# A gated mix of sliding-window attention and a GEGLU on one core: keys of the first two chunks become a seven-product pair, two early loads change queues, VectorE sums become wider

## The chip, the cores and the metric

The kernel runs on one NeuronCore of a Trainium2 chip. Times are device microseconds of one execution. Before the change the median of 8 runs is 725.83 us (725.45 to 727.29). The engines are named as the profile names them: PE (TensorE matmul) with PEld (its weight loads), DVE (VectorE), ACT (ScalarE), POOL (GpSimd) and SP (SyncE, which here only issues DMAs). For this kernel a difference of about 0.2%, 1.45 us, is what a measurement can tell from no change.

## The reference

The input `x` is 2048 tokens by 1024 features in bfloat16. Two branches are computed from it and mixed by a gate per token:

```python
g = sigmoid((x * gate_w).sum(-1, keepdims=True))
a = A(x)          # qkv = x @ wqkv; 32 heads of 32; each token sees 8 keys, 2 apart; softmax; @ wo
b = (gelu(x @ w_gate) * (x @ w_up)) @ w_down      # 1024 -> 3584 -> 1024
return g * a + (1 - g) * b
```

## The kernel before, in words

The tokens are cut into four chunks of 512 (`SC`), and two chunks make a super-chunk (`NSUP` is 2). Everything is kept transposed: `xT(c, kt)` is feature tile `kt` of chunk `c`, 128 features by 512 tokens, and lies in the buffers called `lend`. Chunk 0 comes in as four plain row loads that PE transposes (lines 1252 to 1259). Chunks 1 to 3 come in by DMA transposes, eight per chunk (line 334), which write straight into the transposed form.

PE does nearly all its work in matmuls of 128x128 weights by 128x512 inputs. Most matrix products are done for two chunks together by a Strassen-like scheme of seven half-size products in place of eight (`qkv_pair`, `ffn`, `down`). The seven need sums and differences of quarters of the weights ("forms") and of the inputs (`x_forms`, four DVE instructions a super-chunk, into `tf`). Weight forms are made on DVE: for the feed-forward weights in `wforms` (line 457), for the down weights in `preps` (lines 431 to 436), for query, key and value weights in `qkv_forms` (line 576). The other way, one chunk at a time with all eight products, is `qkv` and, for the queries of chunk 0, `qkv_outer`, whose outer loop runs over the weight tiles as they land. Both use line 496.

The work of the first super-chunk in PE's order (`main`, lines 1243 to 1292): five dummy matmuls (line 298), 32 transposes of chunk 0, queries of chunk 0 (64 matmuls), keys of chunk 0 (64), the gate of chunk 0 (`gate`, 8 small matmuls, line 735), values of chunks 0 and 1 as a pair (112, line 628), a small gate sum (line 759), queries of chunk 1 (64), keys of chunk 1 (64), the gate of chunk 1, then the feed-forward of both chunks (28 steps of 28 matmuls, line 995), and the down and output projections (line 1159) of chunk 0. Then queries, keys and values of chunks 2 and 3, all as pairs, the down projection of chunk 1, and the same again for the second super-chunk.

A feed-forward step f takes PSUM banks A, Bk and Dk. DVE adds twice from PSUM in each step (line 1079, "u2", and line 1058, "up2") and multiplies once (line 1039, "h"). The product called A22 of step f is started on PE two steps later and needs up2 of f.

Attention is on DVE: scores in `scores` (multiply, line 798, and add, line 804, on 128x2048), then a DMA transpose of the sum (line 867), a softmax of small instructions, a DMA transpose back (line 936), the products with the values (line 945) and their sums (lines 953, 958 and 962). It runs in eight half-chunks beside PE's work.

The order of all this is set when the kernel is built. `Weave.run` holds ten streams (`main`, `loads`, `wforms`, `attention` and others) and emits, one at a time, the operation that could start first by the costs written into the code, with a bias per stream and due times (`DUE`) for some. Every engine then executes its own list strictly in that order, so an instruction that waits holds up all that stands behind it on its engine. That holds for DMA issues too: SP issues in order, and there are eight completion semaphores for the DMAs of SP and ACT, taken in turn, so that each issue first waits for the landing of the one eight issues earlier.

Weights pass through a ring of 20 slots of 256 KB (`NG`, `ring`). The queries' and values' weights of super-chunk 0 lie in spare room of `hT` (`qbuf`, `vbuf`). The order of early loads on SP is: two of the four row loads of x (ACT issues the other two), eight tiles of query weights (line 393), eight tiles of key weights (line 328), two loads of 1 MB with the value weights (line 396), the eight DMA transposes of chunk 1 (line 334), and then down and feed-forward weights (lines 355 and 367).

## Time and profile before

| what | value |
|---|---|
| median of 8 runs | 725.83 us |
| profiled execution, its own time | 725.73 us |
| span of that execution in the trace | 723.9 us |
| PE busy | 717.8 us, 99% of the span |
| DVE busy | 598.9 us, 83% |
| ACT busy | 315.2 us, 44% |
| DVE busy from 100 to 200 us | 99.41 of 100 us |
| DMA, mean rate | 238 GB/s |

The span is the time from the first to the last instruction in the trace; the execution's own time is 1.8 us longer. A busy PE is not yet a PE at its best rate, because matmuls overlap, so the spacing of the matmuls has to be looked at too. In the profile a line such as "L496" is line 496 of the kernel before. In a row of the chain or of the timeline the first number is the start in us, the second the duration in us; "x8" is the number of instructions; what stands in brackets is idle time of the engine before them and what ended it.

### The profile page before, as it was taken

The page shows a single profiled execution, that of the slowest core. Times are in us where ns is not written, and L with a number is a line of the kernel's source. Part 1 is how long each engine was busy: PE and PEld are TensorE (multiplying, and loading weights), DVE is VectorE, ACT ScalarE, POOL GpSimd, SP SyncE. Part 2 cuts the span into 40 slices and gives each one's busy share as a digit, 9 for nine tenths or more (in the row PEclk, how much of TensorE's full clock was granted, in tenths as well). Part 3 has the DMA queues.
Part 4 walks back from the last instruction along what each step waited for, and adds up shares of the span by engine and source line. Part 5 has one row for each costly group of instructions (what it writes and reads, how often), then busy time and mean ns, then how long its engine had stood idle before and what let it go on. Part 6 is the DMA issues. An engine that isn't in the chain of part 4 may idle for free.

```text
span 723.9 us, 9982 instructions
## 1 busy us (share of the span) xinstructions
PE 717.8 (99%) x3381; PEld 352.0 (49%) x3381; DVE 598.9 (83%) x898; ACT 315.2 (44%) x535; POOL 71.8 (10%) x128
## 2 busy tenths in 40 slices
PE   8999999999999999999999999999999999999997
PEld 6666644444444444456655444444444444444443
DVE  1799999999999899799599976999999995794200
ACT  2353465556655532035552114567558557110110
POOL 1000434343121100100000000000000000001000
PEclk9999999999999999999999999999999999999999
DMA  8944799989998979945239999786566757999992
GB/s 312 244 142 103 206 360 309 338 255 350 257 235 195 266 243 314 348 132 146 58 98 311 354 325 305 235 186 176 158 178 158 177 156 172 330 316 329 325 309 96
DMA packets 180931, 172.12 MB, mean 238 GB/s; under 512 B 56464, under 2 KB 137360, under 8 KB 180880
## 3 DMA queue, kind: packets, MB, share of 16 engines
q1 hardware_dynamic: 172048, 143.69, 68.3%
q0 software_dynamic: 8544, 27.27, 10.9%
q8 instruction: 26, 0.43, 0.2%
q10 hardware_dynamic: 288, 0.52, 0.2%
q14 instruction: 25, 0.20, 0.1%
HBM read 129.50 MB, written 28.31 MB: 218 GB/s over the span
## 4 chain that ended last, share of the span: by engine, by line
PE 97%; DMA 2%; ACT 0%; DVE 0%; issue 0%
PE ps L995 45%; PE ps L1159 30%; PE ps L628 13%; PE ps L496 8%; DMA ring<-in_B_w_gate_dram 2%; DMA hT<-in_A_x_dram 0%; PE ps L1252 0%; PE ps L735 0%; ACT ost L1194 0%; PE ps L759 0%; ACT hT L1036 0%; ACT m L1049 0%; DVE lend L1259 0%
## 5 line engine op out<-in xcount | busy, mean ns | idle before, releaser
L995 PEld LDWEIGHTS <-ring 128*128 128x128 bf16 x1568 | 153.2, 98 | 185.8 <-issue 1.6
L995 PE MATMUL ps<-lend,ring 128*128 128x512 bf16 x896 | 212.3, 379 | 0.4 <-ACT m L1049 0.4
L995 PE MATMUL ps<-tf,ring 128*128 128x512 bf16 x672 | 164.0, 379 | 0.0
L1159 PE MATMUL ps<-ring,hT 128*128 128x512 bf16 x708 | 160.7, 379 | 0.0
L1159 PEld LDWEIGHTS <-hT 128*128 128x128 bf16 x708 | 69.2, 98 | 83.3
L945 DVE TENSOR_TENSOR xbuf<-xbuf,lend 128x2048 bf16<-128x2048 bf16 x64 | 77.5, 1218 | 6.8 <-DMA xbuf<-xbuf 6.8
L798 DVE TENSOR_TENSOR xbuf<-qo,lend 128x2048 bf16<-128x2048 bf16 x64 | 76.8, 1218 | 0.1
L804 DVE TENSOR_TENSOR xbuf<-xbuf 128x2048 bf16<-128x2048 bf16 x56 | 68.3, 1219 | 0.3
L628 PEld LDWEIGHTS <-ring 128*128 128x128 bf16 x384 | 49.3, 129 | 33.8 <-DMA ring<-in_A_wqkv_dram 0.4
L1024 ACT COPY ps<-ps 128x512 f32<-128x512 f32 x56 | 32.0, 572 | 55.6 <-PE ps L995 55.5
L1067 ACT ACTIVATE gl<-ps 128x512 bf16<-128x512 f32 x56 | 33.5, 598 | 49.5 <-PE ps L995 48.4
L1194 ACT ACTIVATE ost<-ps,omg 128x512 bf16<-128x512 f32 x16 | 11.0, 687 | 100.6 <-PE ps L1159 100.6
L1186 POOL DMA_DIRECT2D out_dram<-ost x24 | 13.0, 540 | 410.4 <-ACT ost L1194 319.1
L1159 PE MATMUL ps<-ring,qo 128*128 128x512 bf16 x192 | 49.3, 379 | 0.0
L466 POOL DMA_DIRECT2D fforms<-ring x56 | 30.5, 546 | 176.1 <-DVE ring L457 168.0
L1039 DVE TENSOR_TENSOR hT<-hT,gl 128x1024 bf16<-128x1024 bf16 x56 | 38.4, 685 | 11.3 <-ACT hT L1036 11.3
L628 PE MATMUL ps<-lend,ring 128*128 128x512 bf16 x208 | 47.3, 380 | 0.0
L953 DVE TENSOR_TENSOR xbuf<-xbuf 128x1024 bf16<-128x1024 bf16 x64 | 42.0, 685 | 0.4
L1079 DVE TENSOR_TENSOR u<-ps,u 128x512 f32<-128x512 f32 x56 | 38.4, 686 | 4.5 <-PE ps L995 3.4
L628 PE MATMUL ps<-tf,ring 128*128 128x512 bf16 x176 | 40.3, 379 | 0.0
L1058 DVE TENSOR_TENSOR hT<-ps,m 128x512 bf16<-128x512 f32 x56 | 38.4, 685 | 1.4 <-PE ps L995 1.3
L1075 ACT COPY u<-ps 128x512 f32<-128x512 f32 x56 | 32.8, 586 | 15.1 <-PE ps L995 15.1
(110 smaller groups left out, 700.1 us busy)
## 6 DMA issues: line engine op xcount, KB each, us to landing
ring<-dforms SPq DMA_DIRECT2D x112, 256.0 KB, 5.0
ring<-in_B_w_down_dram SPq DMA_DIRECT2D x84, 256.0 KB, 4.3
ring<-in_B_w_gate_dram SPq DMA_DIRECT2D x56, 256.0 KB, 4.9
fforms<-ring POOLq DMA_DIRECT2D x56, 256.0 KB, 5.2
ring<-fforms SPq DMA_DIRECT2D x56, 256.0 KB, 4.0
ring<-in_B_w_up_dram SPq DMA_DIRECT2D x42, 256.0 KB, 4.8
ring<-in_A_wqkv_dram SPq DMA_DIRECT2D x32, 256.0 KB, 4.5
ring<-oforms SPq DMA_DIRECT2D x32, 256.0 KB, 5.5
```

The costliest lines, as they stand in the source:

```text
L496: nc.tensor.matmul(banks[bk][:], lhsT=lhsT, rhs=xT(c, kt), start=(kt == 0), stop=(kt == KT - 1))
L628: nc.tensor.matmul(banks[bk][:], lhsT=lhsT, rhs=rhs[:, kt, :], start=(start and kt == 0), stop=(kt == KH - 1), skip_group_check=True)
L798: V(out=w3(box[t]), in0=q_b, in1=k_w, op=ALU.mult)
L804: V(out=w3(box[0]), in0=w3(box[0]), in1=w3(box[t]), op=ALU.add)
L945: return dve(tt(n), taking(("p", t), lambda: V(out=w3(box["p", t]), in0=w3(box["ab"]), in1=v_w, op=ALU.mult)), [("qkv", c, 2, t), abo] + ( ...
L953: V(out=s4(t)[:, t % 2], in0=w3(box["p", t])[:, 0:4], in1=w3(box["p", t])[:, 4:8], op=ALU.add)
L995: nc.tensor.matmul(banks[bk][:], lhsT=wv[:, k, fl * P:(fl + 1) * P], rhs=rhs[:, k, :], start=(start and k == 0), stop=(k == KH - 1), skip_ ...
L1039: yield dve(tt(2 * SC), lambda f=f: nc.vector.tensor_tensor(out=hrow[:, f, :], in0=hrow[:, f, :], in1=gl[f][:], op=ALU.mult), [e, ev[f, "g ...
L1058: ev[f, "up2"] = dve(tt(SC, True), lambda f=f: nc.vector.tensor_tensor(out=hs(f, 1), in0=v3(banks[Bk[f]][:]), in1=v3(m5[f][:]), op=ALU.add ...
L1067: nc.scalar.activation(out=gl[f][:, SC:2 * SC], in_=banks[A[f]][:], func=ACT.Gelu_apprx_tanh)
L1079: e = dve(tt(SC, True), lambda f=f: nc.vector.tensor_tensor(out=u2[f][:], in0=banks[Dk[f]][:], in1=u2[f][:], op=ALU.add), [o, ev[f, "u2"]])
L1159: nc.tensor.matmul(banks[bk][:], lhsT=l, rhs=wv[:, i, :], start=(start and k == 0), stop=(q == last and i == 1), skip_group_check=True)
```

## The change

The keys of chunks 0 and 1 are computed as a pair by `qkv_pair`, like the values; the two calls of `qkv` for keys go. For that, the forms of the key weights are made on DVE, and all of chunk 1's input and its forms have to be there before the pair. `main` has the gates of both chunks right after the queries of chunk 0, then the key pair, both gate sums, the value pair and the queries of chunk 1. The eight DMA transposes of chunk 1 are issued by ACT, behind its last copy of chunk 0's transposes. The eight key weight tiles are issued by POOL, behind the landing of query weight tile 5. The value weights are issued by SP once the last transpose of chunk 1 has landed. The forms of query, key and value weights are made two tiles at a time (128x1024 where it was 128x512), and so are the first sums of the value products (128x2048 where it was 128x1024). The dummy matmuls at the start become six of 512 columns and three of 128. The last step of `qkv_outer` is issued bank by bank. Biases, due times and the look-ahead of the planner have other values, and the order in which scores go over the tiles is `TORD`.

```diff
-    AHEAD = 11.0
+    AHEAD = 17.53
-    DUE = (88.5, 308.0)
+    TORD = (0, 1, 4, 5, 2, 3, 6, 7)
+    DUE = (102.09, 307.15)
-    for i in range(5):
-        nc.tensor.matmul(banks[7][:], lhsT=warm[:, 0:P], rhs=warm, start=True, stop=True)
+    for n_ in [SC] * 6 + [P] * 3:
+        nc.tensor.matmul(banks[7][:, 0:n_], lhsT=warm[:, 0:1].to_broadcast([P, P]), rhs=warm[:, 1:2].to_broadcast([P, n_]),
+                         start=True, stop=True)
...
+    def early_x():
+        for kt in range(KT):
+            yield Op("ACTQ", (P * SC * 2, 1.3), lambda kt=kt: nc.scalar.dma_start_transpose(
+                out=xT(1, kt), in_=x[SC:2 * SC, kt * P:(kt + 1) * P]), [("pt", NST - 1, 1)], key=("x", 1, kt))
+
+    def early_k():
+        for i in range(KH):
+            for kt in (i, i + KH):
+                def fn(kt=kt):
+                    nc.gpsimd.dma_start(out=ring_take(("wqkv", 0, 1, kt)).rearrange("p (k n) -> p k n", k=1), in_=qkv_src(1, kt, 1))
+                yield Op("POOL", (P * GR * 2, 0.8), fn, [("wqkv", 0, 0, 5)], key=("wqkv", 0, 1, kt), pre=ring_pre, after=(kt == 0))
...
-        yield from load_qkv(0, 1, range(KT))
         yield Op("SP", (KT * P * D * 2, 1.0), lambda: [nc.sync.dma_start(out=vbuf[:, hf * KH:(hf + 1) * KH], ...
-                 [("pt", NST - 1, 1)], key=("wqkv", 0, 2))
-        yield from load_x(1, [])
+                 [("x", 1, KT - 1)], key=("wqkv", 0, 2), after=True)
...
-            for which in QVK if sup else (2,):
+            for which in QVK if sup else (1, 2):
...
-                    for kt in range(KH):
+                    for kt in range(0, KH, 2):
...
-        def sums(t, m):
+        def sums(t, deps):
             def fn():
-                V(out=s4(t)[:, t % 2], in0=w3(box["p", t])[:, 0:4], in1=w3(box["p", t])[:, 4:8], op=ALU.add)
+                p0, p1 = flat(("p", t)), flat(("p", t + 1))
+                lo, hi = [_win_ap(p0[:, k * n // 2:k * n // 2 + 1], [[p1.offset - p0.offset, 2], [1, n // 2]]) for k in range(2)]
+                V(out=p0.rearrange("p (u n) -> p u n", u=2), in0=lo, in1=hi, op=ALU.add)
+            return dve(tt(n), fn, deps)
...
         yield from qkv_outer(0)
-        yield from qkv(0, 1)
         yield from gate(0)
+        yield from gate(1)
+        yield from qkv_pair(0, [1])
+        yield from gate_sum(0)
+        yield from gate_sum(1)
         yield from qkv_pair(0, [2])
-        yield from gate_sum(0)
         yield from qkv(1, 0)
-        yield from qkv(1, 1)
-        yield from gate(1)
         yield from halo(1)
...
-    w.run([(0.0, main()), (0.0, loads()), (0.0, late_x()), (0.88, wforms()), (0.0, down_forms()), (0.1, x_forms()), (1.43, qkv_forms()),
-           (1.3, preps()), (0.13, attention()), (0.36, scores())])
+    w.run([(0.0, main()), (0.0, loads()), (0.0, early_x()), (0.0, early_k()), (0.0, late_x()), (0.01, wforms()), (0.0, down_forms()), (0.1, x_forms()), (0, qkv_forms()),
+           (0.56, preps()), (0.05, attention()), (0.14, scores())])
```

As built, the lists of the engines change so: PE has 12 matmuls fewer in all (16 of 128x512 for the keys fewer, four dummies more); DVE has 898 instructions before and 849 after; ACT has five copies more and issues eight transposes; POOL issues eight loads more; SP issues 16 DMAs fewer. In the later part of SP's list, six of the eight DMA transposes of chunk 3 stand among the first down weight loads of chunk 0, and two a little further on; before, seven of them stood ahead of those loads.

## The prediction

> **What bounds the kernel now.** I read the page first, then the chain of waits in order of time, then the timeline of the first 40 us, the windows around chunk 1's transposes, and those transposes by themselves.
>
> ```profile
> PE 717.8 (99%) x3381; PEld 352.0 (49%) x3381; DVE 598.9 (83%) x898; ACT 315.2 (44%) x535; POOL 71.8 (10%) x128
> ...
> PE 97%; DMA 2%; ACT 0%; DVE 0%; issue 0%
> ```
>
> ```profile
> 7.79 27.79 PE ps L496 x128
> 35.58 0.55 PE ps L735 x8
> 36.13 24.33 PE ps L628 x112
> 60.46 0.18 PE ps L759 x8
> 60.63 27.78 PE ps L496 x128
> 88.41 0.55 PE ps L735 x8
> 88.96 5.30 PE ps L995 x24
> ```
>
> The chain is PE almost alone, and PE runs without holes: 128 matmuls in 27.79 us is 0.217 us each, 112 in 24.33 the same, and that spacing holds through the feed-forward. So a matmul that goes is worth 0.217 us as long as PE is never made to wait. Whether it is, is decided in the first 90 us, where almost everything moves.
>
> ```profile
> 6.89 1.31 ACT L1257 COPY lend<-ps 128x512 bf16<-128x512 bf16 x2 [0.27 <-PE ps L1252]
> ...
> 14.97 14.86 SPq L334 DMA_TRANSPOSE lend<-in_A_x_dram  x8
> ...
> 20.30 2.05 ACT L542 CAST qo<-ps 128x512 bf16<-128x512 f32 x4 [12.10 <-PE ps L496]
> ```
>
> ```profile
> 15.00:22.00 7.00, 7.00 (x34) 4.66 (x33) 1.41 (x3) 1.71 (x4) 0.00 (x0) 1.00 1.05 386
> 22.00:24.50 2.50, 2.50 (x13) 1.67 (x12) 1.07 (x2) 0.93 (x2) 0.00 (x0) 1.00 1.59 142
> 24.50:31.30 6.80, 6.80 (x33) 4.53 (x32) 6.49 (x17) 2.34 (x4) 0.00 (x0) 1.00 0.66 138
> ```
>
> The last two numbers of a window are the DMA share and GB/s. The DMA engines are full up to 22 us at 386 GB/s; where transposes and plain loads overlap (22 to 24.5) the rate falls to 142, and the transposes alone take 6.8 us. ACT has a hole of 12.1 us before 20.30; DVE's first weight forms start at 24.81, when the value weights land. The transposes by themselves, those of chunk 1 and then those of chunks 2 and 3, which share the DMA engines with other traffic:
>
> ```profile
> L334 SPq DMA_TRANSPOSE lend<-in_A_x_dram x8: 1258/1262/3423, 15.0 to 28.6; - x8
> ...
> DMA to landing us min/median/max: 2.6/3.6/10.2
> ```
>
> ```profile
> L334 SPq DMA_TRANSPOSE lend<-in_A_x_dram x16: 1144/1252/1784, 188.7 to 248.3; - x16
> ...
> DMA to landing us min/median/max: 3.1/5.8/7.2
> ```
>
> **The change part by part**, against the profiled execution's 725.73 us (span 723.9 and 1.8 around it; 0.1 under the median, so nothing is corrected for that).
>
> *Matmuls.* Keys for two chunks: 128 before, 112 as a pair, 16 x 0.217 = **-3.46 us**, all on the path.
>
> *Gates.* Two gates together take 0.98 (the chain at 313.49) against 2 x 0.55, two sums 0.24 (at 387.25) against 2 x 0.18: -0.24; and two changes of matmul kind fewer at about 0.06: **-0.35**.
>
> *Start.* The query matmuls start at 7.79, after the seventh copy of chunk 0's transposes. Now the sixth is enough, 0.43 us earlier (the copies alternate at that step), but PE's own 32 transposes end at 7.6 (4.11 and 3.47 long). The four dummies more (one 0.427, three 0.107 each by the same rate) may push the first transpose, now at 4.11, by up to 0.3. The second query weight lands at 8.87 (issued 2.13, 6.7 to landing), and 56 matmuls follow it: the queries cannot end before 8.87 + 12.12 = 20.99, against 21.64. Between +0.3 and -0.65: **-0.3**, half the better end. The Trainium skill ("TensorE: Matmul & The Clock Gate", Part 1) has the array at half clock until about 3.4 us of activity; the trace agrees, 0.427 from one dummy to the next and 0.216 later. By that page longer dummies let the transposes run at full clock and this term would be -0.65.
>
> *Chunk 1's input, the new wait.* The gate of chunk 1 now stands at 21.3 + 0.55 = 21.9 on PE and needs all eight transposes; before, they had until 60. On ACT they follow the copy that ends at 8.20, and each has to wait for the landing of one query weight: the first goes at 8.2, the second after 8.87, ends at about 9.5 at the row's usual 1.26, the last starts at 9.5 + 6 x 1.26 = 17.0. From ACT no row shows a transpose; SP's are the nearest. Landing: 2.6 at best gives 19.6, no wait. The median among other traffic, 5.8, gives 22.8; half a microsecond more for slots of query weights that now share the engines: 23.4, a wait of **+1.5 us**. The high end by work: query weights until 13.0 (4.1 us after 8.87), keys 5.4 (eight loads at 386 GB/s), transposes 6.8, together 8.9 + 16.3 = 25.2, and once more the 2.5 us of the mixed window: 27.7, a wait of 5.8. I take the median row since it has the same mix. The Trainium skill ("DMA: Bandwidth & Descriptors", "Issuing engines are not separate DMA queues") speaks against the change: issuing from another engine saves issue time only, all run on the same 16 engines and interleave. The trace agrees as to the share, 1.05 from 15 to 22 us. By that page alone everything ends together, at the 25.2 of the work, and the term would be +3.3.
>
> Behind the waiting ACT stand five query copies, wanted from 20 us. If the issues take 1.26 they end at 18.3 and cost nothing; at the worst issue of 3.42 for two of them 22.6, still under the wait for the last landing. Behind the waiting SP stand the value weights: issued at 23.4, two loads of 1 MB at 386 GB/s, landed by 31. Their first reader on DVE is not due before 31 and the value pair starts at 48; hidden, and 17 us would have to go before it costs.
>
> *Key weights on POOL.* POOL has nothing else there. They start at the landing of query weight 5, 11.5 to 13, at 0.55 us each (the row of its 256 KB stores), the last at 16 to 17; landing 5.2 (same row) to 7.7 (its slowest median): 21.5 to 25. PE needs them first after both gates, 24.3, and their second half of forms at 26: **0**, up to +1.
>
> *DVE.* Added to the first 90 us: eight key forms at 0.60 and eight additions from PSUM at 0.60, 9.6 us; one copy less, -0.6; value forms 16 x 0.335 to 8 x 0.60, -0.5. Later, 48 query, key and value forms at 0.335 become 24 at 0.60, -1.6, and 64 value sums at 0.60 become 32 at 1.136, -2.2. (These are start-to-start spacings; the rows' means are 0.08 longer since neighbours overlap.) Does it reach PE? The first point is up2 of step 0. Work ahead of it in DVE's list, its kinds times spacings: before 70.1, now 77.4 us. Before, it ended at 97.1, so DVE had idled 27.0, of that 21.0 before 24.81, and PE's A22 came at 99.55. Now DVE starts on chunk 1's forms at about 17, not 24.8; I lay the list beside PE's (copies of the queries until 22.6, second key weights 24, value weights 31, additions that wait for the pair at 32, 44 and 57) and get 18.3 idle, plus 0.7 for instructions that follow the one they depend on at once: ready at 96.4. A22 stands at 97.4 by the terms so far. Steps 1 and 2 have 1.7 and 2.0, from step 3 to the end of the stage 3 to 4. With an earlier input DVE gains less than PE, so DVE takes what would go past 3.4 us of gain. **+0.3**, between 0 and +2.
>
> *Later stages.* PE's list is the same from the feed-forward on. Chunk 3's transposes now go among the down weights at about 250 to 262 us: eight issues, 10 us of SP. Down weights land 4 to 18 us ahead of use there, 0 to +1, taken 0. What PE waits today in mid-kernel (0.5 at 176 us) may go or stay.
>
> Sum: -3.46 - 0.35 - 0.3 + 1.5 + 0.3 = **-2.3**; 725.7 - 2.3 = **723.4 us**.
>
> **Rivals.**
>
> *Transposes land late (the other side).* Place: the gate of chunk 1. Every microsecond after 21.9 costs one; the gain without it, 4.1, is gone at 26.0, and from 27.5 on the kernel is over 0.2% slower. For it: 142 GB/s in the mixed window, issues of 3.42 us, a landing of 10.2. Against: both came behind 2 MB of value weights on one queue, which now come later. At 27.7 the wait is 5.8, DVE has time again, and the sum is -4.1 + 5.8 = +1.7: 727.4; a landing a microsecond later, 728.4.
>
> *No wait at all.* Landing by 21.9, as at 188.7 us with 4.9 to 5.8 a piece if the query weights are not slowed. Then 4.1 less 0.7 that DVE takes: 722.3 to 721.6.
>
> *DVE becomes the bound at the start of the feed-forward.* If key weights land at 25 or later and the additions slip with them, up2 of step 0 is 1 to 2 us late and PE stands there. For it: 9 us more work on DVE in a stretch where it is busy 18.8 to 19.4 of each 20 us already (windows from 40 to 100 us). Against: an instruction that follows at once the one it depends on starts 0.72 after it where others take 0.60 (lines 431 and 433 at 91.85 and 92.57), and DVE's whole list has 82 of these, 139 before. 724.7 to 725.5.
>
> **How the numbers follow.** About 0.2%, 1.45 us, is what can be told: under 724.4 is faster, over 727.3 slower. The forecast's own case (wait of 0.5 to 2.5) 0.43; no wait 0.20; DVE as bound, or a wait of 2.5 to 5.5, 0.21; late transposes beyond that, 0.16. Faster 0.63, same 0.21, slower 0.16. The range runs from the no-wait case, 721.5, to the edge of the late one, 727.3; outside lie 0.16 above and little below.
>
> **What would show it.** In the chain: 352 matmuls of L517 and L650 before the first L1017 (where 368 of L496 and L628 stood before L995), the first L1017 near 86.8 (88.96 before). PE idle of 1 to 2 us before the second gate (L757), released by a DMA into lend; the last transpose on ACT's queue issued near 17, landed near 23.4. PE's spacing 0.217 beyond. DVE's first x form near 17, up2 of step 0 (L1080) before A22. It is wrong if PE waits over 4 us for that gate, or waits in several places after 90 us, or if ACT's copies of the queries start after 23.

## The result, and the profile after

The changed kernel takes 731.66 us (median of 13 runs, 727.89 to 733.56) against 725.68 us (36 runs of the kernel before beside them, 724.87 to 727.29): a ratio of 1.0073, 95% interval 1.0063 to 1.0083. It is slower by about 6 us, where 2.3 us faster was forecast. The profiled execution took 729.28 us with a span of 727.5 (725.73 and 723.9 before), so it lies 2.4 us under its median; before, the two were within 0.1. The spread itself is a result: 5.7 us, against 2.4 before.

The page of the kernel after, engine totals and shares of the chain:

```profile
PE 716.4 (98%) x3369; PEld 347.8 (48%) x3369; DVE 597.9 (82%) x849; ACT 318.2 (44%) x540; POOL 76.3 (10%) x136
...
PE 77%; issue 14%; DMA 3%; DVE 2%; POOL 2%; ACTq 1%; ACT 1%; SPq 0%; POOLq 0%
```

PE has 12 matmuls fewer and is busy for 1.4 us less, but the span grew by 3.6: PE now waits. Where it waits is in the chain in order of time (start, duration, what; of the kernel after):

```profile
15.34 9.74 DMA lend<-in_A_x_dram
25.12 0.98 PE ps L757 x2
26.10 25.41 PE ps L650 x112
51.75 24.33 PE ps L650 x112
...
317.19 1.16 DVE ring L595 x2
318.35 1.14 DVE lend L502
319.48 1.14 DVE tf L503
321.26 1.29 DVE ring L595 x2
323.61 0.64 DVE zt L763
325.19 65.77 PE ps L650 x304
```

Two places have links that are not PE. At the start a transpose of chunk 1's input takes 9.74 us to land, and behind it the key pair's 112 matmuls take 25.41 us where the value pair's 112 take 24.33. Near 317 us, in the pair of chunks 2 and 3, VectorE stands between PE's links. The list of PE's waits (engine, line, releaser: us in total, times, longest) names the same:

```profile
PE ps L757 <- DMA lend<-in_A_x_dram: 2.1, 2, 1.6
PE ps L650 <- ACT u2q L694: 1.4, 1, 1.4
PE ps L650 <- DVE ring L595: 1.3, 1, 1.3
```

The span divides into three stretches, read from the first feed-forward matmul and the first matmul of the third gate:

| | first feed-forward matmul | from there to the third gate | the rest |
|---|---|---|---|
| before | 88.89 | 224.53 | 410.5 |
| after | 89.72 | 224.48 | 413.3 |

So after minus before is +0.8 in the start, nothing in the first feed-forward, +2.8 in the rest. The start was to gain 2.6 and lost 0.8.

**The start.** PE's timeline (start, duration, what, idle before it and what ended it):

```profile
21.05 0.61 PE L757 MATMUL ps<-lend,gcol 128*32 128x512 bf16 x8
22.01 0.59 PE L757 MATMUL ps<-lend,gcol 128*32 128x512 bf16 x5 [0.34 <-DVE qo L565]
23.14 0.38 PE L757 MATMUL ps<-lend,gcol 128*32 128x512 bf16 x1 [0.54 <-DMA lend<-in_A_x_dram]
25.12 0.98 PE L757 MATMUL ps<-lend,gcol 128*32 128x512 bf16 x2 [1.60 <-DMA lend<-in_A_x_dram]
26.03 2.81 PE L650 MATMUL ps<-lend,ring 128*128 128x512 bf16 x7
```

Two gates without a wait take 0.98; here the key pair begins 4.98 after the first gate does. That is a delay of 4.0 us. Then the first key matmuls go at half rate, five of them 426 to 441 ns apart where 217 is usual: another 1.1. The last transposes are the cause. The first piece, 0.34 us, is ended by a copy of queries on VectorE and not by a DMA; it costs nothing as long as the transposes land after it. By line, with issue times and then the time from issue to landing:

```profile
L344 ACTq DMA_TRANSPOSE lend<-in_A_x_dram x8: 1140/1285/1750, 6.5 to 16.7; - x8
...
DMA to landing us min/median/max: 4.4/6.7/9.7
```

They were issued as forecast (last at 16.66), but landed at 13.4 to 25.5 us. The windows of the kernel after (window, length, busy of PE, PEld, DVE, ACT, POOL, granted clock, DMA share, GB/s) show why:

```profile
12.00:18.00 6.00, 6.00 (x30) 3.97 (x29) 1.94 (x2) 0.00 (x0) 4.30 (x9) 1.00 1.33 299
18.00:20.00 2.00, 2.00 (x11) 1.35 (x10) 0.51 (x1) 0.35 (x1) 0.00 (x0) 1.00 0.63 65
20.00:22.00 2.00, 1.67 (x14) 0.68 (x13) 1.34 (x3) 2.00 (x5) 0.00 (x0) 1.00 1.01 177
22.00:26.00 4.00, 1.85 (x8) 0.30 (x7) 3.70 (x6) 0.19 (x1) 0.00 (x0) 0.86 0.78 210
```

Between 18 and 20 us only 65 GB/s arrive, while four transposes and key loads are outstanding. The key loads' packets of 4096 bytes, which take 171 ns in the median, take 1.5 to 2.4 us at 17.9 (15 of them) and 0.9 to 1.4 at 20.5. Before, the same thing happens at 22.4 to 24.6 (105 GB/s there, with packets of the transposes of 0.9 to 2.2 us), when PE needs none of that data.

**The later stage.** PE in the pair of chunks 2 and 3, after:

```profile
315.18 1.95 PE L650 MATMUL ps<-lend,ring 128*128 128x512 bf16 x8
318.41 3.65 PE L650 MATMUL ps<-tf,ring 128*128 128x512 bf16 x16 [1.28 <-DVE ring L595]
321.89 1.89 PE L650 MATMUL ps<-lend,ring 128*128 128x512 bf16 x8
325.19 1.02 PE L650 MATMUL ps<-lend,ring 128*128 128x512 bf16 x4 [1.41 <-ACT u2q L694]
```

Before, these matmuls followed one another without a gap:

```profile
314.40 1.95 PE L628 MATMUL ps<-lend,ring 128*128 128x512 bf16 x8
316.19 3.62 PE L628 MATMUL ps<-tf,ring 128*128 128x512 bf16 x16
319.64 5.46 PE L628 MATMUL ps<-lend,ring 128*128 128x512 bf16 x24
```

Now two stalls stand there: 1.66 and 1.79 us from the start of one matmul to the start of the next, where 0.217 is usual.

### The profile page after: what moved, and what is told of

The parts are those of the page before. It is cut to its first block, busy times and chain, and to the rows that moved or that the text cites. A ratio compares the mean times of both kernels' runs of the same rounds, so it can differ in the third digit from the quotient of the medians.

```text
span 727.5 us, 9918 instructions
## 1 busy us (share of the span) xinstructions
PE 716.4 (98%) x3369; PEld 347.8 (48%) x3369; DVE 597.9 (82%) x849; ACT 318.2 (44%) x540; POOL 76.3 (10%) x136
## 4 chain that ended last, share of the span: by engine, by line
PE 77%; issue 14%; DMA 3%; DVE 2%; POOL 2%; ACTq 1%; ACT 1%; SPq 0%; POOLq 0%
PE ps L1017 36%; PE ps L1182 22%; PE ps L650 16%; PE ps L517 2%; DMA lend<-in_A_x_dram 1%; POOL fforms L487 1%; DMA hT<-in_A_wqkv_dram 1%; ACTq L344 1%; POOL out_dram L1215 1%; DMA ring<-in_B_w_gate_dram 1%; DVE ring L595 0%; DVE ring L478 0%; DMA out_dram<-ost 0%; DVE u L1101 0%; ACT L925 0%
## 5 line engine op out<-in xcount | busy, mean ns | idle before, releaser
L1017 PEld LDWEIGHTS <-ring 128*128 128x128 bf16 x1568 | 153.4, 98 | 185.8 <-issue 1.1
L1017 PE MATMUL ps<-lend,ring 128*128 128x512 bf16 x896 | 212.3, 379 | 0.6 <-ACT m L1071 0.6
L1017 PE MATMUL ps<-tf,ring 128*128 128x512 bf16 x672 | 164.0, 379 | 0.0
L650 PEld LDWEIGHTS <-ring 128*128 128x128 bf16 x496 | 63.9, 129 | 47.9 <-issue 4.2
L826 DVE TENSOR_TENSOR xbuf<-xbuf 128x2048 bf16<-128x2048 bf16 x56 | 68.2, 1217 | 0.2
L650 PE MATMUL ps<-lend,ring 128*128 128x512 bf16 x272 | 63.0, 384 | 1.4 <-ACT u2q L694 1.4
L650 PE MATMUL ps<-tf,ring 128*128 128x512 bf16 x224 | 51.3, 379 | 1.3 <-DVE ring L595 1.3
L977 DVE TENSOR_TENSOR xbuf<-xbuf 128x2048 bf16<-128x2048 bf16 x32 | 39.0, 1218 | 0.1
```

What stands on the lines that cost most here:

```text
L650: nc.tensor.matmul(banks[bk][:], lhsT=lhsT, rhs=rhs[:, kt, :], start=(start and kt == 0), stop=(kt == KH - 1), skip_group_check=True)
L826: V(out=w3(box[0]), in0=w3(box[0]), in1=w3(box[t]), op=ALU.add)
L977: V(out=p0.rearrange("p (u n) -> p u n", u=2), in0=lo, in1=hi, op=ALU.add)
L1017: nc.tensor.matmul(banks[bk][:], lhsT=wv[:, k, fl * P:(fl + 1) * P], rhs=rhs[:, k, :], start=(start and k == 0), stop=(k == KH - 1), skip_ ...
```

## The experiments

All ratios are to the kernel before, run beside each. Four edits come back, so they are shown once and named.

`narrow`: for the second super-chunk, the weight sums are made one tile at a time (128x512) as before the change:

```diff
-            t = tt(D)
+            step = 1 if sup else 2
+            t = tt(step * D // 2)
...
-                    for kt in range(0, KH, 2):
+                    for kt in range(0, KH, step):
...
-                        dep = raw_keys(c, which, (kt, kt + KH, kt + 1, kt + 1 + KH))
+                        dep = raw_keys(c, which, [k for u in range(step) for k in (kt + u, kt + u + KH)])
```

`zt`: the gate's transposes on VectorE lose their head start in the planner where it did harm. `late gate`: the second gate moves behind the key pair. `plain`: every DMA transpose becomes a plain DMA of the same bytes from the same queue, so the data is not turned and the output is not the reference's.

```diff
-        e = dve(0.63, lambda: nc.vector.transpose(out=zt[:], in_=banks[i][:]), [o], bias=0.7)
+        e = dve(0.63, lambda: nc.vector.transpose(out=zt[:], in_=banks[i][:]), [o], bias=0.7 if c < 2 else None)
```

```diff
         yield from gate(0)
-        yield from gate(1)
         yield from qkv_pair(0, [1])
         yield from gate_sum(0)
-        yield from gate_sum(1)
         yield from qkv_pair(0, [2])
+        yield from gate(1)
         yield from qkv(1, 0)
+        yield from gate_sum(1)
```

```diff
-            yield Op("ACTQ", (P * SC * 2, 1.3), lambda kt=kt: nc.scalar.dma_start_transpose(
-                out=xT(1, kt), in_=x[SC:2 * SC, kt * P:(kt + 1) * P]), ...
+            yield Op("ACTQ", (P * SC * 2, 1.3), lambda kt=kt: nc.scalar.dma_start(out=xT(1, kt), in_=x[1 * SC + kt % 4 * P:1 * SC + (kt % 4 + 1) * P, kt // 4 * SC:(kt // 4 + 1) * SC]), ...
```

### Is it the clock? Filling PE's hole

```diff
+    FILL = {5: 4, 6: 4, 7: 5}
...
+                    for _ in range(FILL.get(kt, 0) if c == 1 else 0):
+                        nc.tensor.matmul(banks[fb[0]][:], lhsT=warm[:, 0:1].to_broadcast([P, P]),
+                                         rhs=warm[:, 1:2].to_broadcast([P, SC]), start=True, stop=True)
```

> Thirteen idle matmuls (128x512 of zeros, into a bank that nothing uses then) stand in TensorE's list before the second gate's sixth, seventh and eighth matmul, where it waited 0.92 and 1.98 us in the trace of after; every other engine's list is as in after. Theory A, the hole closes the clock gate: the five matmuls behind it that came 426 to 441 ns apart come 216 ns apart; every run has a mean granted clock of 1.000, the median falls from 731.7 to 727 to 729 us and the spread from 5.7 to under 2.5 us. Rival B, the clock closes elsewhere (behind the stalls at 316.7 and 323.4 us, say, or by the load of the whole run): the clock stays at 0.994 to 0.998, the median at 730 to 733 us. If the fillers delay the stage themselves (13 x 0.216 = 2.8 us against 2.9 us of waiting), the key pair starts up to 1 us later than the 26.03 us of after.

Measured: 731.63 us (728.73 to 734.4, 6 runs), 1.008 [1.0057, 1.0102]. PE with the fillers:

```profile
25.57 0.38 PE L765 MATMUL ps<-lend,gcol 128*32 128x512 bf16 x1 [0.33 <-DMA lend<-in_A_x_dram]
...
27.40 1.95 PE L651 MATMUL ps<-lend,ring 128*128 128x512 bf16 x8
```

Eight key matmuls now take 1.95, the full rate. But neither the median nor the spread moved. In the runs of the kernel after, the mean granted clock falls as the time grows (1.000 at 727.89 us, 0.994 to 0.995 above 731); with the fillers a run of 731.53 us has 1.000. The half-rate matmuls are a small share, and the theory that the lost clock explains the slow median and the spread fell.

### Moving the second gate away

> The second gate stands behind the key pair instead of before it. The pair's first 24 matmuls (5.2 us) read only the first four of chunk 1's transposed tiles, which landed by 15.8 us in after. Theory C, the transposes alone are late: TensorE goes from the first gate into the key pair at 21.5 us without a wait, the first FFN matmul comes near 86 us (89.89 in after), the clock stays at 1.000 and the time is 724 to 726 us, what is left of the loss being in the pair of chunks 2 and 3. Rival D, the key weights are as late as the transposes (GpSimd's eight loads landed from 15.6 to 24.6 us, the seventh at 23.8): the pair's first products wait 2 to 3 us for them at 21.5 us, its forms come 1 us later still, the first FFN matmul comes at 87.5 to 89.5 us, the clock closes in some runs, and the median is 727 to 731 us.

The edit is `late gate` alone. Measured: 757.77 us (753.75 to 758.83, 5 runs), 1.0432 [1.0411, 1.0453]. PE, and then ACT, of this kernel:

```profile
21.83 0.87 PE L650 MATMUL ps<-lend,ring 128*128 128x512 bf16 x3
24.89 1.30 PE L650 MATMUL ps<-lend,ring 128*128 128x512 bf16 x5 [2.19 <-DMA ring<-in_A_wqkv_dram]
```

```profile
74.35 0.59 ACT L694 COPY u2q<-ps 128x512 f32<-128x512 f32 x1 [18.85 <-DVE zq L767]
```

Two things are learnt. First, the key weights are next in line: with the gate gone PE waits 2.2 us for them. Second, a trap: `u2q`, a copy in the value pair, waits 18.85 us for `zq`, an instruction of the gate that has nothing to do with values. The two share buffers: `zt` of the gate and `u2q` have one tag with two buffers, and the order of emission put `zt` ahead of `u2q`. PE stood 17.03 us (from 57.95) for it. The rest of this kernel's loss is in the second super-chunk, where the time from the third gate to the end is 419.9 (413.3 in the kernel after).

### The two late stalls, one at a time

> Only the weight forms of chunks 2 and 3 are made by sums of one ring slot and half the width again, as in before; the pair of chunks 0 and 1 keeps the wide ones. Theory E, a wide sum is held to touch every slot between the two that it reads or writes: the first form starts when its two weights are there, near 308 us, and not behind the eighth (312.04 us in after); the first form product no longer waits for the in-place difference two forms later, and TensorE's stall of 1663 ns at 316.7 us goes: 1.4 to 1.9 us less than after at the same clock. Rival F, the weights come late (their loads are issued from 301.6 us, in before from 298.4), so that the forms are late whatever their width: a stall of over 1 us stays between 315 and 320 us and the time moves by less than 0.7 us. The stall at 323.4 us (1793 ns) stays in both, or shrinks where VectorE gets to the gate's transposes sooner. Median 729 to 731 us, since the second gate's hole stays.

> The transposes of the gates of chunks 2 and 3 lose the bias of 0.7 that puts them behind other VectorE work; those of chunks 0 and 1 keep it. Theory G: the pair's copies into the buffers u2 wait until the gates' transposes have left those buffers (first copy at 324.56 us behind the gate's column copy of 324.27 in after), and TensorE's stall of 1793 ns at 323.4 us is that wait: it goes, for 1.3 to 1.8 us less at the same clock. Rival H, VectorE is late there altogether: the transposes (0.71 us each) push the forms back, the stall at 316.7 us (1663 ns) grows by as much as the other shrinks, and the time moves by less than 0.5 us. Median 729 to 732 us either way, since the second gate's hole stays.

> Both edits of the pair of chunks 2 and 3: its weight forms one ring slot wide again, and its gates' transposes without the bias. Up to 300 us every engine's list is as in after. Theories E and G together: no TensorE gap over 0.7 us between 314 and 330 us (1663 and 1793 ns in after, 609 ns at 323 us with narrow forms alone), the second gate's hole at 22 us stays, and the time is 726 to 727.5 us with a spread under 2.5 us, since the wide spread of after comes from these stalls. Rival M, VectorE's sums there are late by their number (24 more instructions): a gap of 1 us or more comes back between 314 and 330 us and the median is 728 us or more.

| kernel | us (lowest to highest, runs) | ratio | rest of the span from the third gate |
|---|---|---|---|
| `narrow` | 728.05 (727.0 to 729.8, 5) | 1.0036 [1.0023, 1.0048] | 410.6 |
| `zt` | 729.4 (728.11 to 730.38, 6) | 1.0051 [1.0039, 1.0063] | 413.0 |
| both | 727.74 (726.92 to 729.46, 6) | 1.0027 [1.0014, 1.0039] | 410.9 |

VectorE's first form of the chunk 2 and 3 weights, in the kernel after and then with `narrow`:

```profile
312.04 0.69 DVE L595 TENSOR_TENSOR ring<-ring 128x1024 bf16<-128x1024 bf16 x1 [3.12 <-DMA ring<-in_A_wqkv_dram]
```

```profile
308.81 0.41 DVE L601 TENSOR_TENSOR ring<-ring 128x512 bf16<-128x512 bf16 x1
```

The wide form reads four weight tiles, in ring slots 5 and 12, and 6 and 16. Its access pattern is one start, one step and a count. In the built program its waits are

```
wide form: reads slots 5, 12, 6, 16   waits for loads into 5, 6, 12, 16 and also 13, 14
```

Its own four tiles had landed by 309.37; the last of all it waits for landed at 311.96. The pattern is tracked as the whole stretch between its first and last slot. The same happens on the other side: a weight load of PE from slot 11 waits for an in-place difference that writes slots 5 and 12 and ends at 318.3. With narrow forms this stall is gone, PE in `narrow`:

```profile
316.29 1.95 PE L656 MATMUL ps<-lend,ring 128*128 128x512 bf16 x8
318.07 3.40 PE L656 MATMUL ps<-tf,ring 128*128 128x512 bf16 x15
...
323.65 3.61 PE L656 MATMUL ps<-lend,ring 128*128 128x512 bf16 x16 [0.23 <-ACT u2q L700]
```

The other stall is the shared buffer again: in the kernel after, ACT's copy waits for the gate's VectorE work.

```profile
324.56 0.59 ACT L694 COPY u2q<-ps 128x512 f32<-128x512 f32 x1 [3.55 <-DVE zq L767]
```

`zt` alone takes that one away, but the first stall grows:

```profile
319.88 3.43 PE L650 MATMUL ps<-tf,ring 128*128 128x512 bf16 x15 [2.58 <-DVE ring L595]
```

In that profile the first wide form waited for its loads until 313.52 (after 4.43 us idle, 3.12 in the kernel after), so the rest of the span is shorter by 0.3 us only, which is what rival H forecast. The two edits were not tried in a profile with the same landings, so what `zt` is worth by itself is not separated from that. `narrow` alone brings back 2.7 of the 2.8 us: in its profile the second stall has shrunk to 0.61 us from one matmul's start to the next, since VectorE comes to the gate's work sooner. With both edits PE has no gap over 0.44 us from 314 to 330 us, and 2.4 us come back; that `zt` adds something to `narrow` is not shown. What is left is the start: in the profile of both edits PE waits 3.0 and 0.8 us for the last transposes, and ten matmuls go at half rate.

### Filling the hole with the late stalls gone

> Fillers in the second gate's hole and both edits of the pair of chunks 2 and 3, nothing else. If the clock loss comes from the hole and the wide spread from the two later stalls, no half-rate matmuls are left anywhere, every run has a clock of 0.999 or more, the median is 725 to 726.5 us and the spread under 1.5 us: 1 to 2.5 us below the same kernel without fillers (727.7 us, 726.9 to 729.5). If the clock closes for another reason, clocks of 0.995 to 0.998 stay and so does the median of 727.7 us.

`narrow`, `zt` and the fillers: 729.09 us (727.6 to 730.71, 6 runs), 1.0049 [1.0035, 1.0062], not better than the 727.74 without fillers. In its profile the transposes landed as late as 28.68, and PE's key pair starts at 30.97. So the hole follows the landing, which differs from profile to profile, and not the clock.

### Other orders at the start

Key weights ahead of the transposes, on SP, in place of POOL:

```diff
+        yield from load_qkv(0, 1, [k for i in range(KH) for k in (i, i + KH)])
...
-    w.run([(0.0, main()), (0.0, loads()), (0.0, early_x()), (0.0, early_k()), ...
+    w.run([(0.0, main()), (0.0, loads()), (0.0, early_x()), ...
```

> The key weights of chunk 0 go by SyncE's queue right behind the query weights instead of GpSimd's queue behind the sixth of them; the pair of chunks 2 and 3 is left as in after. Theory I, GpSimd's loads are what holds the transposes up: in after 18 to 20 us moved little on either queue, and its 512 packets of 4096 bytes took 271 ns each, 8.7 us of the sixteen engines, where SyncE's packets of 2048 bytes took 84 to 96 ns. The query weights end near 13.2 us, the keys follow in 5.5 us, and with the transposes' own 5.7 us of packets everything is there by 21 to 23 us: the second gate waits under 1.5 us in all, its last matmul comes before 24 us, and the median is 728 to 730 us, what is left being the stalls at 316 and 323 us. Rival J, bytes are what counts: the keys now come before the transposes and the last transpose lands at 25 us or later, the hole is as long as in after or longer, and the time is 730 us or more.

750.46 us (747.28 to 752.59, 5 runs), 1.0334 [1.0312, 1.0356]. The keys landed in time (13.4 to 21.0), but the eight completion semaphores are shared by SP and ACT, and an issue waits for the DMA eight earlier. With eight more on SP the transposes could only begin at 12.07, and ACT came to its query copies at 23.39. PE waited 2.5 us for these and, in the re-planned lists, up to 2.4 us at a time in the feed-forward and 6.6 us for a `u2q` copy in the second super-chunk. Theory I fell: without loads from GpSimd the last transpose landed at 24.71, and from 18 to 19.5 us 73 GB/s arrived, with packets of 2048 bytes that took 1.4 us.

> Four edits together: the key weights by SyncE's queue, the second gate behind the key pair (its transpose without the bias), and the two edits of the pair of chunks 2 and 3. If theories I, E and G hold, TensorE goes from the first gate into the key pair at 21.5 us and waits nowhere over 1 us up to the FFN, whose first matmul comes at 86 to 87 us (89.89 in after, 88.96 in before); no gap over 0.7 us between 314 and 330 us; clock 1.000, median 721.5 to 724 us, below before. If the key weights or the first transposes are still late (rivals D and J), the key pair waits 1.5 us or more in its first products, the FFN starts at 88 to 89 us, and the median is 725 to 728 us.

The same with `late gate`, `narrow` and `zt` (from chunk 1 on): 734.69 us (733.1 to 736.65, 4 runs), 1.0126 [1.0109, 1.0143]. The wait for ACT's query copies stays in front of the first gate, 3.0 us here. From 18 to 19.5 us 52 GB/s arrived.

> The second gate behind the key pair once more, with the gates' transposes free of the bias and with narrow forms for chunks 2 and 3; the loads stay as in after. Theory G on the 17 us stall of the first kernel of this kind (its transpose of the second gate ran at 73.2 us, 23 us behind the gate's matmuls of 50 us, and TensorE stood from 57.9 to 75.0): the stall is gone, no wait over 1.2 us comes between 30 and 90 us. The key pair still waits 2 to 3 us for the key weights near 22 us (theory D); the first FFN matmul comes at 87.5 to 89 us, and the median is 724.5 to 727 us. If the stall had another cause, it stays and the time is above 740 us.

`late gate`, `narrow`, and no head start for the gates' transposes: 730.05 us (729.56 to 732.2, 5 runs), 1.007 [1.0058, 1.0082]. The 17 us stall is gone and the feed-forward starts at 88.51, 1.2 us earlier than in the kernel after, yet its first part takes 228.87 us where the kernel after takes 224.48. VectorE's list was planned anew, and PE waits at several places for its results.

> As the kernel before it, and GpSimd's loads of the key weights wait for the second query weight instead of the sixth (landed 8.77 and 11.53 us in after), so that they are issued 2.5 to 3 us earlier; all key forms but the first stand behind VectorE's copies of the queries. Theory N, the keys are late because they start late: they land by 20 to 22 us, TensorE goes into the key pair with less than 1 us of waiting, the query matmuls are not held up (their last weight landed at 13.2 us, 5 us ahead of its use at 18.7), the first FFN matmul comes at 85.5 to 87.5 us, the clock is 1.000, and the median is 721.5 to 724.5 us. Rival O, the engines' total is the limit (query weights, keys and transposes together): the keys are there only 0 to 1 us sooner, or the query weights are later and TensorE waits inside the queries; FFN at 87.5 us or later, median 725 us or more.

The same with POOL's key loads released by the second query weight in place of the sixth, and key forms behind the query copies: 738.23 us (734.34 to 742.28, 6 runs), 1.0174 [1.0147, 1.0201]. Releasing the loads earlier brought them in only 1.2 us sooner (16.4 to 23.4), one issue on ACT took 4.5 us, PE waited 2.2 us for ACT's query copies, and a new VectorE order left PE waiting 6.1 us in the feed-forward.

> No transposing transfers before 60 us: chunk 1's rows come by four plain loads on SyncE's queue behind the key weights (which go by SyncE too), and TensorE transposes them as it does chunk 0's, in 32 instructions of some 56 ns behind the queries, with eight copies shared by VectorE and ScalarE; the second gate stands behind the key pair, and the pair of chunks 2 and 3 has both edits. Theory P, the stretch of packets of 1 to 2.8 us between 17.9 and 22.9 us comes where transposing transfers and plain loads meet: it is gone, the engines move 380 GB/s up to 18 us, keys and rows are there by 19 us, and TensorE pays 1.8 us for its transposes and at most 1.5 us for the copies behind them. The key pair starts at 23.5 to 24.5 us, the first FFN matmul comes at 86.5 to 88 us, the clock stays at 1.000, the runs agree within 1.5 us, and the median is 722.5 to 726 us, above that only if the FFN stage waits in several places as in the other kernels with a new start. Rival Q, the stall has nothing to do with transposes: packets of over 1 us stay, the loads land at 21 us or later, and TensorE waits over 2 us.

Chunk 1 by four row loads on SP and 32 transposes on PE behind the queries, and the keys on SP; `late gate`, `narrow`, no head start, and key forms behind the query copies as in the kernel just told of:

```diff
+        yield from load_qkv(0, 1, [k for i in range(KH) for k in (i, i + KH)])
+        yield from rows_x()
...
+                def go(pt=pt, j=j, k0=k0):
+                    for kk in range(KH):
+                        nc.tensor.transpose(out=pt[:, kk, :], in_=xrow1(j, k0 + kk, 1), identity=ident)
```

733.4 us (730.1 to 736.19, 6 runs), 1.0097 [1.0075, 1.012]. Without DMA transposes there is no stretch of slow packets at the start: loads landed from 13.6 to 22.3. The key pair begins at 24.11. But the shared buffer costs again,

```profile
34.19 2.32 PE L691 MATMUL ps<-lend,ring 128*128 128x512 bf16 x7 [2.09 <-ACT u2q L735]
```

and PE waits 3.6 us for VectorE in the feed-forward, whose stage is 231.0 long.

### Undoing the pair, keeping the moves

> The key pair is undone: chunk 0's and chunk 1's keys by 64 matmuls each, in the order of the stages of before, so that chunk 1's input is first read at 35 us; its transposes stay on ScalarE's queue and the key weights on GpSimd's, the start and the wide sums stay, and the pair of chunks 2 and 3 has both edits. It has 16 matmuls more (3.46 us). Theory K, the pair as placed costs more than its matmuls save, by the hole and the closed clock: no hole before 35 us but a wait of at most 3 us for the key weights at 21 us, the first FFN matmul at 87.5 to 89 us, and a median of 724 to 726 us, 1 us or more below the kernel with the pair and both edits. Rival L, the pair's saving outweighs its hole: this one is 1 us or more slower than that kernel, at 727 us or more. A wait for the key weights is possible in both.

Keys as twice 64 matmuls in the stage order of before, `narrow`, no head start; loads on ACT and POOL as after: 734.54 us (734.15 to 735.0, 4 runs), 1.0122 [1.0109, 1.0136]. PE waits 2.3 and 0.7 us for key weights, and 13 matmuls go at half rate. Its feed-forward starts at 94.78, 5.9 us later than in the kernel before, which has as many key matmuls: the moved loads cost even without the pair. Taking the pair away makes it worse, against theory K: with it (`narrow` and `zt`) the time is 727.74. Of these 6.8 us, 3.46 are the matmuls and 2.9 a longer first feed-forward (227.38) under the list planned anew, so this run does not say what the wait alone is worth.

### What makes the DMA engines stand

> As after, but GpSimd's first key load waits for the last transpose of chunk 1's input instead of the sixth query weight, so that the transposes meet only the last query weights. Theory P, the meeting of GpSimd's 4096-byte packets and the transposes stalls the engines: without the key loads the eight transposes are limited by their issue (1.3 us each from 6.5 us, the last at 16.7) and the last one lands by 19 us, against 25.47 in after, with no packets over 1 us before that. The key weights then come from 19 to 25 us, so TensorE waits for these instead, and the time says nothing. Rival Q, transposes stall by themselves or with any load: the last one lands at 21 us or later, with packets of over 1 us before 20 us.

```diff
-                yield Op("POOL", (P * GR * 2, 0.8), fn, [("wqkv", 0, 0, 5)], ...
+                yield Op("POOL", (P * GR * 2, 0.8), fn, [("x", 1, KT - 1)], ...
```

Key loads only behind the last transpose. 755.36 us (2 runs), 1.0407 [1.0389, 1.0425], since now the keys are late (9.3 us of PE's waits) and the re-planned lists add others (8.0 us for one `u2q` copy). It is meant for the transposes alone:

```profile
L344 ACTq DMA_TRANSPOSE lend<-in_A_x_dram x8: 1140/1282/2401, 6.6 to 17.9; - x8
...
DMA to landing us min/median/max: 2.6/3.9/7.0
```

Issued 1.2 us later at the end, the last lands at 20.53 and not at 25.47; the median from issue to landing falls from 6.7 to 3.9, and no data packet takes over 1 us. The landing lies between theory P's 19 and rival Q's 21 us. One issue took 2.40 us, and from 16 to 18 us hardly anything moved (13 GB/s), so transposes alone do not keep the engines busy either; but nothing else was waiting then.

> The kernel before with every transposing transfer replaced by a plain one of the same bytes into the same place (chunk inputs in 128x512 pieces, the attention's turns as copies), so that its data are not turned and what it computes from them is another thing; instructions and their order stay. It is the base for the three beside it. Its transposing transfers end at 31.3 us, 4 us ahead of their first use on TensorE, and the attention waits for them off TensorE's path: the time stays within 1 us of 725.6, the first FFN matmul near 89 us. If it is more than 2 us faster, transposing transfers cost the kernel before something too.

> After with the same replacement. Theory P, the stretch of slow packets comes where transposing transfers meet plain loads: no packets over 1 us from 17 to 23 us, the chunk's input lands by 18 us and the key weights by 22, TensorE waits under 1.5 us at the second gate and the key pair together, no matmul at half rate before 60 us, and the first FFN matmul comes at 85.5 to 87.5 us. The two stalls of the pair of chunks 2 and 3 (3 us) stay, so the median is 722.5 to 726 us, with a spread of several us from those stalls. Rival Q, bytes are the limit: the key weights land at 24 us or later all the same, TensorE waits over 2.5 us, the FFN starts after 88 us.

With plain copies everywhere, in the kernel before and in the kernel after:

| kernel | us (lowest to highest, runs) | ratio |
|---|---|---|
| before, `plain` | 725.70 (725.08 to 727.34, 10) | 1.000 [0.999, 1.001] |
| after, `plain` | 724.84 (723.94 to 725.57, 10) | 0.9985 [0.9975, 0.9994] |

The same two microseconds in the windows of after with `plain`:

```profile
18.00:20.00 2.00, 2.00 (x11) 1.33 (x10) 0.00 (x0) 0.00 (x0) 0.00 (x0) 1.00 1.00 389
```

389 GB/s where it was 65, with the same bytes from the same queues. In the kernel before, the mixed window from 22 to 24.5 us goes from 142 to 354 GB/s. To the kernel before, plain copies are worth nothing; to the kernel after, 6.8 us at the median, and the spread falls from 5.7 to 1.6 us. Of the 4.9 us between the two profiles, 3.3 are in the start (the feed-forward begins at 86.45) and 1.6 in the rest (411.7): the weights of chunks 2 and 3 land sooner too, by 307.13 us, and the wide forms no longer stop PE, while the `u2q` stall of 1.72 us stays. So the loads beside plain copies do not bring the stretch of long packets about, and neither do the transposes with only the last query weights beside them; transposes and key loads together do, from GpSimd's queue or from SP's. The Trainium skill ("DMA: Bandwidth & Descriptors", "Rules for kernel authors") says that a transpose next to ordinary DMAs needs nothing. That speaks of what has to be kept apart for the data's sake; these runs show what it costs in time, 65 in place of 389 GB/s for two microseconds.

### What is left without each of the causes

> The kernel with both edits of the pair of chunks 2 and 3 (727.7 us), with the same replacement. Theories P, E and G together: the first FFN matmul at 85.5 to 87.5 us, 224 to 225 us from there to the third gate, 406 to 407 from that to the end, and a median of 720 to 723 us, 2.5 to 5 us below the kernel before with the same replacement: the saving that the prediction put at 2.3 us is there once the transposing transfers are off. Rival S, VectorE gives it back in the FFN: its stage takes 226 us or more and the median is 723.5 us or more.

> The same again, and the second gate, the key pair and the sums of chunk 1's input read chunk 0's input, the key pair the query weights, so that nothing at the start waits for an early load. First FFN matmul at 84.3 to 85.3 us, which is 88.9 less 3.5 of matmuls, 0.3 of joined gates and 0.3 to 1.2 of an earlier start. The difference to the kernel without this is what is left of waiting for key weights: 1 to 2.5 us by theory P, over 3 us by rival Q. If the FFN's stage is as long as in the kernel without it, the time follows the FFN's start one for one; if it is longer by 1 us or more, VectorE takes the gain back (rival S).

> The mended kernel with plain transfers (723.5 us), but the gates' transposes are written into a buffer of the tag gl, which nothing uses at that time, instead of the tag u2 of the pair's copies, and they keep the bias of 0.7 everywhere, as in after. Theory G in its plain form: TensorE's 1.57 us at 29.3 us, where the copy into u2 waited for the gate's column copy of 30.85, are gone, and no gap over 0.7 us comes near 320 us although the transposes stand as late there as in after; the first FFN matmul comes at 84.9 to 85.5 us (86.47) and the median is 722.0 to 722.8 us. If it was VectorE's lateness and not the buffer, a wait of over 1 us stays at 29 us, and with the bias back one of 0.6 us or more near 322 us, and the median is 723.3 us or more.

The third of these has `narrow` and gives the gate's `zt` a buffer of another tag, with its head start kept:

```diff
-        zt = work.tile([P, SC], F32, tag="u2", bufs=2, name="zt")
+        zt = work.tile([P, 2 * SC], BF16, tag="gl", bufs=3, name="zt")[:].bitcast(F32)
```

| kernel, all with `plain` | us (lowest to highest, runs) | ratio |
|---|---|---|
| `narrow`, `zt` | 723.52 (723.35 to 724.1, 6) | 0.9970 [0.9958, 0.9982] |
| the same, the second gate, the key pair and x forms read chunk 0's data for chunk 1's, the pair query weights for keys | 723.16 (722.99 to 723.22, 4) | 0.9962 [0.9947, 0.9977] |
| `narrow`, own buffer for `zt` | 721.74 (721.45 to 722.24, 5) | 0.9942 [0.9928, 0.9956] |

With plain copies the early waits are worth only 0.4 us more. The shared buffer is worth more: in the first kernel of the table ACT still waits at the start,

```profile
30.19 0.59 ACT L698 COPY u2q<-ps 128x512 f32<-128x512 f32 x1 [3.38 <-DVE zq L771]
```

and with its own buffer no wait of PE over 0.9 us is left. PE's timeline at the start, and its waits, of the last kernel:

```profile
21.41 1.05 PE L761 MATMUL ps<-lend,gcol 128*32 128x512 bf16 x16
22.39 1.95 PE L654 MATMUL ps<-lend,ring 128*128 128x512 bf16 x8
```

```profile
PE ps L308 <- DVE xbuf L306: 0.9, 1, 0.9
PE ps L1020 <- ACT m L1074: 0.6, 1, 0.6
```

Its feed-forward starts at 85.00 and its first part takes 224.74. Of the three expectations, the first missed its 720 to 723 us by 0.5 (the rest of the span took 410.9, near the 410.5 of the kernel before, and not 406 to 407), the second its 1 to 2.5 us, and the third kernel came out below its range. None of these computes the reference, so no version that does was found that beats the kernel before; real transposes with narrow forms and the own buffer were not tried.

## Why the prediction was wrong, point by point

The change does about what its parts were forecast to do when nothing is in the way: the last kernel above is 3.96 us faster than the kernel before with the same plain copies (721.74 against 725.70). The sum of the terms without the new wait was -3.8. That the two agree so well is in part luck: the start gained 3.7 (85.00 against 88.66) where the terms say 4.1, and the rest of the span gained 0.3 that no term has. Two steps failed.

*Chunk 1's input, the new wait* (+1.5, at most 5.8). The mechanism was right and was named: a wait before the second gate, released by a DMA into `lend`. The size was wrong. In the profile it is 4.0 us (4.98 less 0.98), and 1.1 us of half-rate matmuls that were in no term, together 5.1; in place of the last landing at 23.4, it was 25.47 here and 28.68 in another kernel's profile. The mistake was to take the median landing of SP's transposes beside other traffic. The row that mattered had been shown in the prediction itself, 142 GB/s in the window where transposes and loads overlap. It was read as the price of an overlap of 2.5 us and used for the high end only, whereas the change makes that overlap the rule: eight transposes amid eight query and eight key loads. The Trainium skill's rule cited there ("DMA: Bandwidth & Descriptors", "Issuing engines are not separate DMA queues") would have made it +3.3, nearer than the row.

*Later stages* ("PE's list is the same from the feed-forward on", taken 0, at most +1). Measured +2.8 in the profile. The step looked at PE's list and at SP's, and only at transfers. But the wide VectorE forms and the head start of the gates' transposes also act in the second super-chunk. There they wait for what they do not read (slots between two slots, 1.66 us), or make others wait through a shared buffer (1.79 us). None of this is in the lists' lengths. `narrow` takes the first stall away and most of the second with it (413.3 to 410.6 for the rest of the span); the buffer of its own takes the second away where the head start stays (410.2, with plain copies).

At the profile these are the whole difference: 723.4 forecast and 729.28 measured is 5.9. The terms ahead of the feed-forward sum to -2.6, which puts its first matmul at 86.3; the 86.8 that the prediction names, and its 97.4 for A22, stand about half a microsecond later than its own terms. It came at 89.72, 3.4 later: 3.6 more of wait and half rate than forecast, less 0.3 that the start did better. The late stage adds 2.8, and the 0.3 for VectorE was not needed.

The other steps:

- *Matmuls* (-3.46) and *Gates* (-0.35): held. 352 matmuls stand before the first L1017; the value pair's 112 take 24.33, spacing 0.217; two gates take 0.98.
- *Start* (-0.3): the second query weight landed at 8.77 and the first gate began at 21.05, for 20.99 as the earliest end forecast: -0.6, near the better end. The 32 transposes took 2.44 us where they took 3.47, as the better of the two estimates had it.
- *ACT's query copies at no cost*: held; they began at 19.65, before the last landing. A query copy on VectorE did hold the second gate for 0.34 us, which the late transposes hide. In three of the other orders they came after 23 and did cost 2.2 to 3.0.
- *Value weights hidden*: held; issued at 25.49 and landed at 33.53 (31 forecast). VectorE waited 1.94 for them, PE not.
- *Key weights on POOL* (0): held, but only since the gate waited longer. They landed up to 24.55, inside the forecast 21.5 to 25; with the gate moved, PE waited 2.2 us for them.
- *DVE* (+0.3): held. The first x form began at 15.95 (about 17 forecast). The first part of the feed-forward keeps its 224.5 us even when it starts at 85.0 (224.74), so the rival in which DVE becomes the bound is refuted for this list. For newly planned lists it is not: 228.87 and 231.0.
- *Transposes land late* was the rival that came closest, given 0.16. It alone (5.1 in place of 1.5) would give 727.0 in the profile; the late stage made the other part.

What stays open: the median lies 2.4 us above the profile. The start's hole varies from run to run (feed-forward starts from 89.7 to 93.6 in profiles of six kernels with the same early list, two of them with fillers), and with plain copies the spread is 1.6 us, so landings are the likely cause. But the late stalls may vary too: `zt` alone has a median 2.3 us below the kernel after (6 runs) with a profile only 0.1 below, and the slowest runs have no trace. Why the DMA engines stand when transposes meet loads was not settled either.

## What to carry to other kernels

A wait that a change adds on purpose should be sized by the worst row of the same mix of transfers, not the median, since transposes amid plain loads had stretches of microseconds in which little moved. When an instruction is made wider over buffers that are not neighbours, or an operation is moved ahead in a planned order, list what it now waits for and whose buffer it reuses: such waits appear far from the edit, and in the stage that the diff does not seem to touch. An order that saves time at the start is worth nothing until the list of the engine behind it is planned as well as before.

## What the runs showed of the hardware

- Eight DMA transposes of 128 KB amid plain loads: stretches of about 4 us (17.9 to 21.9 here) in which packets of 4096 bytes take 0.9 to 2.4 us where the median is 0.171, and 65 GB/s for two microseconds in place of 389. With the key loads behind the transposes no data packet takes over 1 us; with plain copies in the transposes' place two do (1.2 us at most) and the rate stays up. With the loads on SP's queue the stretch is there too, but shorter (52 and 73 GB/s from 18 to 19.5 us). Its length differs from profile to profile.
- PE went to half rate after waits of 0.34, 0.54 and 1.60 us with single matmuls between them (granted clock 0.86 from 22 to 26 us, 0.54 from 26 to 28.5): five matmuls at 426 to 441 ns. The Trainium skill ("TensorE: Matmul & The Clock Gate", Part 1) has the clock fall after an idle window of about 3.4 us; here the idle time was 2.5 us in three pieces, and 13 filler matmuls between them kept the rate (granted clock 1.00 from 20 to 30 us).
- A DMA issue on ACT waited for the landing of one issued on SP eight places earlier: the first transposes were issued at 6.49 and 8.79, just behind query weights that landed at 6.47 and 8.77. Moving loads between the two queues does not free one from the other.
